# A new order of all pieces, and the last 128 tokens cut at column 352, in a fused attention and SoLU layer

## The chip, the cores and the metric

The kernel runs on one core of one Trainium2 chip. The time is device time in microseconds. Of the kernel before there are three timed runs (178.30, 178.34 and 178.52 us, median 178.34 us) and one profiled execution, from which every view below is taken.

## The reference

Eight batches of eight heads go through a linear attention (no softmax: `k^T v` first, then `q` times that), an RMS norm per head, and then a SoLU layer: a matmul, `h * softmax(h)`, a layer norm, a second matmul.

```python
batch, n_heads, seq, head_dim = (8, 8, 576, 64)     # q, k, v
n_tokens, d_model, d_ff = (4608, 512, 1024)         # w_in, w_out, g_ln

kv = np.einsum('bhsd,bhse->bhde', k, v)
out = np.einsum('bhsd,bhde->bhse', q, kv)
rms = np.sqrt(np.mean(out * out, axis=-1, keepdims=True) + 1e-06)
x = out / rms * g_norm            # then to (batch * seq, heads * head_dim)

h = x @ w_in
e = np.exp(h - np.max(h, axis=-1, keepdims=True))
solu = h * e / (np.sum(e, axis=-1, keepdims=True) + 1e-09)
mu = np.mean(solu, axis=-1, keepdims=True)
var = np.mean((solu - mu) ** 2, axis=-1, keepdims=True)
return ((solu - mu) / np.sqrt(var + 1e-06) * g_ln) @ w_out
```

## The kernel before

The 4608 tokens are nine chunks of 512: chunks 0 to 7 take 512 of the 576 rows of one batch each, and chunk 8 the 64 rows that are left of each batch. A chunk passes through these pieces, whose names are used from here on (the first number is always the chunk or batch):

- `q`, `k`, `v` load a batch (DMAs that POOL issues). `kv_mm.b` is the 72 small matmuls of `k^T v`, and `kv.b.x.part` are the six copies that bring its two banks to SBUF in bf16 (`kv_copy`, recorded at L229; VectorE, or ScalarE where the order says `:act`).
- `qT` turns `q`: for chunks 4 to 8 by a transposing DMA on SyncE's queue, before that by TensorE.
- For each half `hf` of the heads: `o_mm.c.hf` (16 matmuls, 64 for chunk 8; they need `qT` and all copies of `kv`), two squares `sq.c.hf.z` on ScalarE, `oa.c.hf` that adds them (VectorE or POOL, L460), `s_mm.c.hf` (one matmul, the mean over a head, L465), `ln` and `ex` on ScalarE (the inverse root, L472 and L476) and `x.c.hf.z` on VectorE (two instructions each, L489).
- For each of eight blocks `f` of `d_ff`: `h.c.f` (four matmuls of 128x512, L532; in two parts for chunks 0 to 2), `exp.c.f` on ScalarE (L539), `u.c.f` = `h * e` on VectorE (L543), `usq.c.f` = `u * u` (ScalarE or POOL), and for each pair of blocks `es.c.n`, the sum of two `e` (POOL, L551).
- VectorE folds these in halves: `ua.c.0` (2048 columns), `ua.c.1`, `ua.c.2`, the same for `usqa`, and one `esa` (all L575). `sums.c` (16 matmuls, L594) takes the three statistics from them, `turn` and `stats` (VectorE) and `rstd.c` (ScalarE) make the factor of the layer norm.
- `out.c.m` (eight matmuls of 128x512 in two parts, L651) is the second matmul for 128 tokens, `ob.c.m` scales it by `rstd` (`scale`, L239 on ScalarE, L241 on VectorE), `store.c.m` writes it out (two DMAs of 64 rows on SyncE's queue, L679; chunk 8 one DMA, L675). The last 128 tokens, `out.8.3`, are done in two column parts `x` = 0 and 1 with a bank, a scale and a store each (`out_half`, `scale_half`).
- `warm.i` are matmuls on zeros whose result nobody reads; `WARM` gives their numbers.

Nothing is scheduled at run time. The string `ORDER` lists all 919 pieces; `Plan.emit` walks it and calls each piece's function, so it is the program order of every engine at once (`:act`, `:pool` choose an engine where there is a choice). An engine takes its instructions in that order and waits, in place, for what each one needs. `ROOMS` gives a digit for every buffer in the order of first use: which of the 8 PSUM banks, which of the 4 `ob` tiles, and so on. A piece whose room was another's before waits until the last reader of that one is done: a matmul group for the `u`, `ob`, `x` or `ln` that empties its bank, an `ob` for the landing of the store that last read its tile. `Plan.run` adds one more rule: a piece on POOL also waits for the folds and adds of VectorE (`ua`, `usqa`, `esa`, `oa`) that stand ahead of it in `ORDER`.

Of the kernel before, what the change touches and what calls it, by code (L numbers as in the profile page):

```python
# [35 lines left out]
exp.1.6 h.1.7.0 h.1.7.1 kv_mm.2.0 kv.2.0.1:act u.1.2 kv.2.1.1:act sums.0 out.0.2.0 w_center.2 kv.2.1.2:act kv.2.1.0:act
w_center.7 u.1.1 out.0.2.1 out.0.2.2 turn.0 stats.0 u.1.6 kv.2.0.2:act kv.2.0.0:act usq.1.0 o_mm.2.0 exp.1.7 usq.1.4
w_center.6 u.1.7 rstd.0 sq.2.0.1 sq.2.0.0 oa.2.0 o_mm.2.1 sq.2.1.1 out.0.1.0 sq.2.1.0 out.0.1.1 out.0.2.3 out.0.1.2
ua.1.0 ob.0.2:act s_mm.2.0 out.0.1.3 oa.2.1 ln.2.0 ex.2.0 ua.1.1 out.0.0.0 out.0.0.1 out.0.0.2 s_mm.2.1 ln.2.1
out.0.0.3 qT_mm.3.0 es.1.1 usq.1.7:act ob.0.1 ob.0.0:act out.0.3.0 out.0.3.1 x.2.0.1 x.2.0.0 qT.3.0 ex.2.1 kv_mm.3.0  # L40
# [695 lines left out]
```

## Time and profile before

| | us |
|---|---|
| median of three timed runs | 178.34 |
| the profiled execution, device time | 177.03 |
| its span (first to last instruction of the profile) | 175.3 |
| PE busy | 166.1 |
| ScalarE (ACT) busy | 149.4 |
| VectorE (DVE) busy | 147.9 |
| POOL busy | 106.9 |

The profiled execution is 1.31 us shorter than the median of the timed runs, and 1.7 us of it lie around the span. All places below are in microseconds from the span's start. In a row of the timeline the first number is the start, the second the time until the end of the last of the `xN` instructions of the row, and the brackets hold the idle time of that engine just ahead of the row and what ended it. In the window table each engine has its busy time in the stretch. In groups by line, the two numbers behind the first bar are the busy time in all and the mean of one in ns. PEld are the weight loads of TensorE, which run beside its matmuls.

### The profile page before, as it was taken

The numbers are of one execution on the slowest core, as the hardware profiler recorded it, in microseconds if no ns is written. First come the engines' busy times: TensorE is split into PE (matmuls) and PEld (weight loads), VectorE is DVE, ScalarE is ACT, GpSimd is POOL, SyncE is SP. The second block draws the span as 40 slices with busy tenths as digits, with TensorE's granted clock in tenths as the row PEclk, the third lists the DMA queues.
The fourth block names the chain that finished last, engine by engine and source line by source line (L and its number), as shares of the span: only waits on it lengthen the run. The fifth ranks groups of instructions, "written<-read, shape, count | busy, mean of one in ns | idle before, by whom it ended". The sixth has DMA issues, their size and how long they took to land.

```text
span 175.3 us, 4772 instructions
## 1 busy us (share of the span) xinstructions
PE 166.1 (95%) x1866; PEld 80.4 (46%) x1891; DVE 147.9 (84%) x319; ACT 149.4 (85%) x277; POOL 106.9 (61%) x114
## 2 busy tenths in 40 slices
PE   7899998999999998999999999998999999999992
PEld 2454444556464443445435444453454444444451
DVE  2442959999999999899999999999999989988930
ACT  2027699999999998999999999986989999999742
POOL 7943378999390895658656679699085282508000
PEclk9999999999999999999999999999999999999999
DMA  5999999999999697999999657999895513125666
GB/s 154 264 205 212 208 296 350 208 208 208 208 206 197 144 232 193 162 201 200 166 170 215 156 120 98 196 114 129 165 203 124 118 32 85 42 61 120 148 157 238
DMA packets 34623, 30.27 MB, mean 173 GB/s; under 512 B 16288, under 2 KB 28328, under 8 KB 34600
## 3 DMA queue, kind: packets, MB, share of 16 engines
q0 software_dynamic: 17792, 16.71, 56.9%
q1 hardware_dynamic: 16520, 12.86, 31.2%
q10 hardware_dynamic: 288, 0.39, 0.6%
q8 instruction: 15, 0.25, 0.6%
q14 instruction: 8, 0.07, 0.1%
HBM read 32.51 MB, written 9.44 MB: 239 GB/s over the span
## 4 chain that ended last, share of the span: by engine, by line
PE 65%; DVE 15%; ACT 8%; DMA 6%; issue 3%; SPq 1%; POOL 1%; ACTq 0%; POOLq 0%
PE out_ps L651 27%; PE h_ps L532 23%; DVE u_sb L543 5%; DMA k_sb<-in_k_dram 5%; DVE x_sb L489 4%; ACT e_sb L539 3%; PE warm_ps L300 3%; PE o_ps L448 3%; PE sum_ps L594 2%; ACT osq_sb L233 2%; PE s_ps L465 2%; PE kv_ps L375 2%; DVE kvd L229 2%; PE qt_ps L427 2%; DMA out_dram<-ob_sb 1%
## 5 line engine op out<-in xcount | busy, mean ns | idle before, releaser
L532 PE MATMUL h_ps<-x_sb,w_in_sb 128*128 128x512 bf16 x276 | 67.8, 379 | 0.9 <-DVE u_sb L543 0.2
L651 PE MATMUL out_ps<-w_out_sb,u_sb 128*128 128x512 bf16 x270 | 65.8, 379 | 0.6 <-issue 0.2
L551 POOL TENSOR_TENSOR es_sb<-e_sb 128x512 bf16<-128x512 f32 x36 | 45.4, 1279 | 26.0 <-ACT e_sb L539 11.4
L543 DVE TENSOR_TENSOR u_sb<-h_ps,e_sb 128x512 bf16<-128x512 f32 x72 | 46.8, 684 | 3.1 <-ACT e_sb L539 2.8
L539 ACT ACTIVATE e_sb<-h_ps,zero_t 128x512 f32<-128x512 f32 x72 | 46.9, 696 | 1.2 <-PE h_ps L532 0.9
L532 PEld LDWEIGHTS <-w_in_sb 128*128 128x128 bf16 x288 | 26.9, 98 | 33.1 <-issue 2.9
L651 PEld LDWEIGHTS <-u_sb 128*128 128x128 bf16 x280 | 26.3, 98 | 32.3 <-issue 2.2
L489 DVE SCALAR_TENSOR_TENSOR x_sb<-o_ps,g_sb,rst_sb 128x256 bf16<-128x256 f32 x72 | 30.1, 478 | 5.6 <-ACT rst_sb L482 3.5
L235 POOL TENSOR_TENSOR usq_sb<-u_sb 128x512 bf16<-128x512 bf16 x25 | 26.0, 1055 | 13.2 <-DVE usq_sb L575 8.0
L233 ACT ACTIVATE usq_sb<-u_sb,zero_t 128x512 bf16<-128x512 bf16 x47 | 32.2, 717 | 0.0
L233 ACT ACTIVATE osq_sb<-o_ps,zero_t 128x512 bf16<-128x512 f32 x36 | 22.9, 692 | 3.6 <-PE o_ps L448 3.6
L239 ACT ACTIVATE ob_sb<-out_ps,rstd 128x512 f32<-128x512 f32 (+1 forms) x29 | 19.2, 671 | 2.7 <-DMA out_dram<-ob_sb 1.4
L575 DVE TENSOR_TENSOR usq_sb<-usq_sb 128x2048 bf16<-128x2048 bf16 (+2 forms) x24 | 18.7, 778 | 0.7 <-ACT usq_sb L233 0.5
L229 ACT CAST kvd<-kv_ps 64x128 bf16<-64x128 f32 (+3 forms) x36 | 8.2, 241 | 9.8 <-DVE kvd L229 9.4
L300 PE MATMUL warm_ps<-zeros 128*128 128x512 bf16 x42 | 11.9, 427 | 1.3 <-DVE zeros L255 1.2
L476 ACT ACTIVATE rst_sb<-lss_sb,zero_t 128x512 f32<-128x512 f32 x16 | 11.7, 730 | 0.4
L472 ACT ACTIVATE lss_sb<-s_ps,eps_t 128x512 f32<-128x512 f32 x16 | 11.2, 700 | 0.8 <-PE s_ps L465 0.8
L575 DVE TENSOR_TENSOR ua_sb<-u_sb 128x2048 bf16<-128x2048 bf16 x8 | 11.1, 1383 | 0.0
L322 POOL DMA_DIRECT2D q_sb<-in_q_dram x10 | 7.7, 768 | 3.9 <-PE kv_ps L375 2.3
L322 POOL DMA_DIRECT2D k_sb<-in_k_dram x9 | 6.7, 743 | 4.3 <-DVE usq_sb L575 3.5
L375 PEld LDWEIGHTS <-k_sb 64*64 64x64 bf16 x576 | 6.8, 107 | 5.3 <-issue 3.0
L322 POOL DMA_DIRECT2D v_sb<-in_v_dram x9 | 7.1, 791 | 3.4 <-DMA w_in_sb<-in_moe_w_in_dram 1.7
(64 smaller groups left out, 141.1 us busy)
## 6 DMA issues: line engine op xcount, KB each, us to landing
out_dram<-ob_sb SPq DMA_DIRECT2D x65, 128.0 KB, 2.4
k_sb<-in_k_dram POOLq DMA_DIRECT2D x6, 576.0 KB, 13.7
v_sb<-in_v_dram POOLq DMA_DIRECT2D x6, 576.0 KB, 13.5
q_sb<-in_q_dram POOLq DMA_DIRECT2D x6, 512.0 KB, 15.8
u_sb<-in_moe_w_out_dram POOLq DMA_DIRECT2D x2, 1024.0 KB, 15.3
q_sb<-in_q_dram POOLq DMA_DIRECT2D x4, 256.0 KB, 9.9
w_in_sb<-in_moe_w_in_dram POOLq DMA_DIRECT2D x2, 512.0 KB, 12.0
v_sb<-in_v_dram POOLq DMA_DIRECT2D x3, 288.0 KB, 8.3
```

Source lines behind the costliest of these rows:

```text
L233: nc.scalar.activation(out=dst, in_=src, func=AF.Square, bias=zero_t[:, :])
L235: on[engine].tensor_tensor(out=dst, in0=src, in1=src, op=MUL)
L239: nc.scalar.activation(out=dst, in_=src, func=AF.Copy, scale=by)
L300: nc.tensor.matmul(t[:, :], zeros[:, 0:128], zeros[:, :], start=True, stop=True)
L322: nc.gpsimd.dma_start(t.rearrange("p n j d -> p n (j d)")[:, hs.start // 2:hs.stop // 2], rows_of(src, b, hs, js))
L489: nc.vector.scalar_tensor_tensor(out=t[:, 2 * hf + dh, z], in0=T["o", c, hf, z][:, dh], scalar=g_rep[dh], in1=T["rst", c, hf][:, z], op0=M ...
L532: nc.tensor.matmul(bank(("h", c, f), [128, 512])[:, :], w_in_sb[:, dt, f * 128:(f + 1) * 128], T["x", c][:, dt].rearrange("p a b c -> p (a ...
L539: nc.scalar.activation(out=t[:, f % 2, :], in_=T["h", c, f][:, :], func=AF.Exp, bias=zero_t[:, :])
L543: nc.vector.tensor_tensor(out=t[:, f, :], in0=T["h", c, f][:, :], in1=T["e", c, f // 2][:, f % 2, :], op=MUL)
L551: on[engine].tensor_tensor(out=t[:, n, :], in0=e[:, 0, :], in1=e[:, 1, :], op=ADD)
L575: nc.vector.tensor_tensor(out=to[:, 0:n, :], in0=src[:, 0:n, :], in1=src[:, n:2 * n, :], op=ADD)
L651: nc.tensor.matmul(bank(("out", c, m), [128, d_model])[:, :], T["u", c][:, f, m * 128:(m + 1) * 128], w_out_sb[:, f, :], start=(f == 0), s ...
```

## The change

`ORDER` and `ROOMS` are replaced as a whole: the same pieces in another order, with other rooms, and with other engines for some. ScalarE has 40 `kv` copies where it had 36 (VectorE 20 for 24), VectorE makes 13 of the adds `oa` where it made 11 (POOL 3 for 5) and 12 scales `ob` where it made 8 (ScalarE 25 for 29). `WARM` has 43 matmuls where it had 44, in eight groups for seven. The last 128 tokens are cut at column 352 instead of 256, and their first part is scaled by VectorE, the second by ScalarE, where ScalarE scaled both.

```diff
 ORDER = """
...
-ua.8.0 ua.8.1 usqa.8.0 store.6.0 store.6.2 ua.8.2 usqa.8.1 out.8.2.0 esa.8.0 usqa.8.2 ob.7.0:act store.6.1 store.7.0
...
-ob.8.3.0:act ob.8.3.1:act store.8.3.0 store.8.3.1:act
+store.6.2 ua.8.1 ua.8.2 usq.8.0:act usq.8.5:act usq.8.3:act usqa.8.0 usqa.8.1 out.8.2.0 usqa.8.2 out.7.2.1 out.8.2.1
+ob.7.0:act out.7.1.0 out.7.1.1 ob.7.1 ob.7.3:act store.6.1 store.7.0 sums.8 store.7.3 turn.8 ob.7.2:act out.8.0.0
+out.8.1.0 stats.8 rstd.8 out.8.0.1 ob.8.0 ob.8.2:act store.7.2 out.8.1.1 ob.8.1 store.7.1 store.8.2:act store.8.0
+out.8.3.0 store.8.1 ob.8.3.0 store.8.3.0 out.8.3.1 ob.8.3.1:act store.8.3.1:act
 """
...
 WARM = """
-17 6 2 2 9 7 1
+17 8 2 3 5 5 2 1
 """
...
+    ENDS = (slice(0, 352), slice(352, d_model))
+
     def out_half(x):
-        t = bank(("out", LAST, 3, x), [128, d_model // 2])
+        t = bank(("out", LAST, 3, x), [128, ENDS[x].stop - ENDS[x].start])
         for f in range(NF):
             nc.tensor.matmul(
-                t[:, :], T["u", LAST][:, f, 384:512], w_out_sb[:, f, x * d_model // 2:(x + 1) * d_model // 2],
-                start=(f == 0), stop=(f == NF - 1),
+                t[:, :], T["u", LAST][:, f, 384:512], w_out_sb[:, f, ENDS[x]], start=(f == 0), stop=(f == NF - 1),
             )
 
     def scale_half(engine, x):
         t = kept_tile(("ob", LAST, 3), [128, d_model], FP32)
-        times(engine, t[:, x * d_model // 2:(x + 1) * d_model // 2], T["out", LAST, 3, x][:, :], T["rstd", LAST][:, 3:4])
+        times(engine, t[:, ENDS[x]], T["out", LAST, 3, x][:, :], T["rstd", LAST][:, 3:4])
```

What the new order does is seen engine by engine. The number behind a tile tells buffers of the same name apart; a name such as `DMAHW4_49` in brackets is one of the eight semaphores on which the landings of the DMAs that SyncE and ScalarE issue are counted in turn.

**First place: the wait of `ob.1.1` on ScalarE.** SyncE's queue around the stores of chunk 0, before; `ob_sb_1071` is `ob.0.1`, `ob_sb_1035` is `ob.0.2`, and `ob_sb_1468` is `ob.1.3`:

```order
L435 DMA_TRANSPOSE qT_sb_1254<-q_sb_685 128x16x128 [waits DMAHW1_49,DMASW5_49]
L679 DMA out_0_dram<-ob_sb_1071 64x512 [waits DMAHW2_49,DVE_49]
L679 DMA out_0_dram<-ob_sb_1071 64x512 [waits DMAHW3_49]
L679 DMA out_0_dram<-ob_sb_1035 64x512 [waits DMAHW4_49]
L679 DMA out_0_dram<-ob_sb_1035 64x512 [waits DMAHW5_49]
L679 DMA out_0_dram<-ob_sb_1468 64x512 [waits DMAHW6_49,Activation_49]
```

The queue has the same sequence in the change. What differs is on ScalarE, before; `ob_sb_1525` is `ob.1.1`, the squares into `osq_sb_1494` are `sq.4.0`, those into `osq_sb_1527` are `sq.4.1`:

```order
L239 ACTIVATE ob_sb_1468<-out_ps_1448,rstd_1350 128x512 [waits DMAHW5_49,DMAHW4_49,PE_49]
L233 ACTIVATE osq_sb_1494<-o_ps_1478,zero_t_81 128x2x256 [waits PE_49,Pool_49]
L233 ACTIVATE osq_sb_1494<-o_ps_1476,zero_t_81 128x2x256
L233 ACTIVATE usq_sb_1252<-u_sb_1233,zero_t_81 128x512 [waits DVE_49]
L239 ACTIVATE ob_sb_1525<-out_ps_1470,rstd_1350 128x512 [waits DMAHW5_49,DMAHW4_49,PE_49]
L233 ACTIVATE osq_sb_1527<-o_ps_1500,zero_t_81 128x2x256
L539 ACTIVATE e_sb_1540<-h_ps_1535,zero_t_81 128x512 [waits PE_49]
L472 ACTIVATE lss_sb_1551<-s_ps_1549,eps_t_79 128x512 [waits PE_49]
```

And ScalarE at the same place with the change, where `ob_sb_1529` is `ob.1.1`:

```order
L239 ACTIVATE ob_sb_1469<-out_ps_1440,rstd_1449 128x512 [waits DMAHW5_49,DMAHW4_49,PE_49]
L233 ACTIVATE osq_sb_1498<-o_ps_1480,zero_t_81 128x2x256 [waits PE_49,Pool_49]
L233 ACTIVATE osq_sb_1498<-o_ps_1478,zero_t_81 128x2x256
L233 ACTIVATE osq_sb_1521<-o_ps_1505,zero_t_81 128x2x256 [waits PE_49]
L233 ACTIVATE usq_sb_1259<-u_sb_1251,zero_t_81 128x512 [waits DVE_49]
L239 ACTIVATE ob_sb_1529<-out_ps_1471,rstd_1449 128x512 [waits DMAHW3_49,DMAHW2_49,PE_49]
L539 ACTIVATE e_sb_1553<-h_ps_1548,zero_t_81 128x512 [waits PE_49,Pool_49]
L472 ACTIVATE lss_sb_1561<-s_ps_1559,eps_t_79 128x512 [waits PE_49]
```

`ob.1.1` takes the tile of `ob.0.1` instead of that of `ob.0.2`: it waits for the store that SyncE issues one pair earlier (the pair on DMAHW2 and DMAHW3), and it stands behind one more square. The bank that `s_mm.4.0` writes was that of `out.1.1`, emptied by `ob.1.1`; with the change it is that of `out.1.3`, emptied by `ob.1.3`.

**Second place: the copies of `kv.7`.** VectorE from `kv.7.0.1` to `kv.7.0.0`, before; the tiles `u_sb_2301` are `u.6`, `ua_sb_2458` is `ua.5.0`:

```order
L229 CAST kvd_7_0_1_152<-kv_ps_2333 64x128 [waits PE_49]
L543 TENSOR_TENSOR u_sb_2301<-h_ps_2318,e_sb_2316 128x512 [waits Activation_49]
L601 STREAM_TRANSPOSE sum_ps_2410<-sum_ps_2410 128x128 [waits PE_49]
L229 CAST kvd_7_0_2_153<-kv_ps_2333 64x128
L606 TENSOR_TENSOR w_2447<-sum_ps_2410,factors_94 128x4x2 [waits DVE_49]
L607 MEMSET w_2447 128x4
L609 TENSOR_TENSOR terms_2450<-sum_ps_2410,w_2447 128x12 [waits DVE_49]
L611 TENSOR_REDUCE vare_2452<-terms_2450 128x4 [waits DVE_49]
L575 TENSOR_TENSOR ua_sb_2458<-u_sb_2048 128x2048
L543 TENSOR_TENSOR u_sb_2301<-h_ps_2427,e_sb_2434 128x512 [waits Activation_49]
L543 TENSOR_TENSOR u_sb_2301<-h_ps_2442,e_sb_2329 128x512 [waits Activation_49]
L229 CAST kvd_7_0_0_151<-kv_ps_2333 128x128
```

ScalarE with the change, where all six copies of `kv.7` stand:

```order
L539 ACTIVATE e_sb_2317<-h_ps_2320,zero_t_81 128x512 [waits PE_49]
L229 CAST kvd_7_1_2_156<-kv_ps_2330 64x128 [waits PE_49]
L229 CAST kvd_7_0_0_151<-kv_ps_2327 128x128
L229 CAST kvd_7_1_1_155<-kv_ps_2330 64x128
L229 CAST kvd_7_1_0_154<-kv_ps_2330 128x128
L539 ACTIVATE e_sb_2433<-h_ps_2428,zero_t_81 128x512 [waits PE_49,Pool_49]
L229 CAST kvd_7_0_1_152<-kv_ps_2327 64x128
L239 ACTIVATE ob_sb_2439<-out_ps_2147,rstd_2231 128x512 [waits DMAHW6_49,DMAHW1_49,DMAHW7_49,DMAHW0_49,DVE_49]
L539 ACTIVATE e_sb_2307<-h_ps_2449,zero_t_81 128x512 [waits PE_49]
L539 ACTIVATE e_sb_2433<-h_ps_2460,zero_t_81 128x512 [waits PE_49]
L229 CAST kvd_7_0_2_153<-kv_ps_2327 64x128
```

Three copies leave VectorE, the last of them from behind `ua.5.0` and two `u.6`; on ScalarE the last of the six stands behind `exp.6.3`, `ob.3.2`, `exp.6.6` and `exp.6.2`. `o_mm.7.1` follows `out.4.1` on TensorE in both.

**Third place: `esa.4.0` on VectorE.** Before, with `usqa.3.1` first, then `oa.6.0` (`osq_sb_2107`), `esa.3.0`, `ua.3.2`, and `esa.4.0` (`es_sb_1876`):

```order
L543 TENSOR_TENSOR u_sb_2048<-h_ps_2062,e_sb_2067 128x512 [waits Activation_49]
L575 TENSOR_TENSOR usq_sb_1596<-usq_sb_1596 128x1024 [waits DVE_49]
L460 TENSOR_TENSOR osq_sb_2107<-osq_sb_2107 128x512 [waits Activation_49]
L575 TENSOR_TENSOR es_sb_1650<-es_sb_1650 128x1024
L575 TENSOR_TENSOR ua_sb_1838<-ua_sb_1838 128x512
L575 TENSOR_TENSOR es_sb_1876<-es_sb_1876 128x1024 [waits Pool_49]
```

With the change, where `es_sb_1911` is `esa.4.0` and `osq_sb_2085` is `oa.6.0`:

```order
L543 TENSOR_TENSOR u_sb_2105<-h_ps_2047,e_sb_2065 128x512 [waits Activation_49]
L575 TENSOR_TENSOR es_sb_1911<-es_sb_1911 128x1024 [waits Pool_49]
L460 TENSOR_TENSOR osq_sb_2085<-osq_sb_2085 128x512 [waits DVE_49,Activation_49]
L575 TENSOR_TENSOR ua_sb_1857<-ua_sb_1857 128x512 [waits DVE_49]
L575 TENSOR_TENSOR usq_sb_1590<-usq_sb_1590 128x1024 [waits DVE_49]
L575 TENSOR_TENSOR usq_sb_1590<-usq_sb_1590 128x512 [waits DVE_49]
```

`esa.4.0`, which waits for the last `es.4` of POOL, has moved ahead of `oa.6.0`, for which `s_mm.6.0` waits. On POOL the pieces ahead of it are `es.4.1`, `es.4.0`, `usq.4.1` before, and `es.4.1`, `usq.4.1`, `es.4.0` with the change.

More of the change, by code (lines that the diff above doesn't have):

```diff
@@ L36 @@
[L36 to L40, printed above, removed]
```

137 lines of the change are left out of this document (70 added, 67 removed).

## The prediction

> **What bounds the kernel now.** I read the busy shares first, then the table of windows, then the chain that ended last, to see which stretch has time to give.
>
> ```profile
> PE 166.1 (95%) x1866; PEld 80.4 (46%) x1891; DVE 147.9 (84%) x319; ACT 149.4 (85%) x277; POOL 106.9 (61%) x114
> 60.00:65.00 5.00, 4.95 (x93) 2.38 (x92) 4.86 (x12) 4.92 (x11) 5.00 (x5) 1.00 1.12 231
> 65.00:70.00 5.00, 4.24 (x48) 1.83 (x48) 4.70 (x10) 4.13 (x8) 3.20 (x4) 1.00 0.96 171
> 120.00:125.00 5.00, 4.40 (x50) 1.98 (x50) 5.00 (x9) 3.60 (x9) 2.63 (x3) 1.00 0.91 181
> 150.00:155.00 5.00, 5.00 (x25) 2.29 (x24) 4.45 (x11) 4.75 (x10) 2.27 (x2) 1.00 0.01 3
> 145.61 3.45 PE h_ps L532 x16
> ```
>
> In a window row come the length and then the busy time of PE, PEld, DVE, ACT and POOL; the 1.00 behind them is the granted clock, which is full throughout. The last row, from the chain, is sixteen matmuls in 3.45 us, 0.216 us each. PE is busy in nearly every stretch, and from about 25 us DVE and ACT are too (4.86 and 4.92 of 5 at 60 to 65). So no reordering shortens the work itself: it can give back waits. PE has few of them: two stretches stand out, 65 to 70 (4.24) and 120 to 125 (4.40). The beginning and the last 3 us are the other places.
>
> The Trainium skill's page "Perfetto Trace Analysis", section "Identifying the Most-Contended Engine", says that matmul busy time is a bad measure and that the busy share of the weight loads tells TensorE's headroom. That share is 46% here, so by the page ACT (85%) and DVE (84%) would be the contended engines. The trace agrees only in part: at 0.216 us a matmul without a gap, PE has nothing to give in 150 to 155, while DVE is full where PE is not, in 120 to 125. What the sum would be by the page's rule stands with the third rival.
>
> **The change part by part.** The sum is made against the profiled execution, 177.03 us with a span of 175.3.
>
> *First place, `ob.1.1`.*
>
> ```profile
> 67.52 0.72 ACT L233 ACTIVATE usq_sb<-u_sb,zero_t 128x512 bf16<-128x512 bf16 x1
> 69.08 0.69 ACT L239 ACTIVATE ob_sb<-out_ps,rstd 128x512 f32<-128x512 f32 x1 [0.83 <-DMA out_dram<-ob_sb]
> 69.82 0.38 PE L465 MATMUL s_ps<-osq_sb,head_mean 128*128 128x512 bf16 x1 [0.71 <-ACT ob_sb L239]
> 72.28 1.66 DVE L489 SCALAR_TENSOR_TENSOR x_sb<-o_ps,g_sb,rst_sb 128x256 bf16<-128x256 f32 x4 [0.64 <-ACT rst_sb L476]
> 64.81 1.10 SPq L679
> 66.60 2.37 DMA out_dram<-ob_sb
> ```
>
> ACT stood 0.83 us before `ob.1.1` until the second half of `store.0.2`, issued at 66.60, had landed 2.37 us later; PE lost 0.71 behind it, DVE 0.64. With the change `ob.1.1` waits for `store.0.1`, whose second half is the issue at 64.81: with the same 2.37 us it lands between 67.2 (from the start of that issue) and 68.3 (from its end). ACT reaches `ob.1.1` after `usq.2.0` (end 68.24) and one square more; if that takes as long as `usq.2.0`, at about 68.9. The wait is covered. `s_mm.4.0` no longer depends on it. All three engines are full around this place, so they gain together what the least of them lost: 0.64 us; bounds 0 (another wait comes instead) and 0.83. I take **-0.65**. Next late there is `h.3.6`, whose bank `ob.1.1` now empties: PE does `out.1.1.1`, `out.1.2`, `h.3.2`, `s_mm.4.0` first, more than 3 us of matmuls behind `o_mm.4`, and `ob.1.1` ends in less.
>
> *Second place, `kv.7`.*
>
> ```profile
> 117.58 0.32 DVE L601 STREAM_TRANSPOSE sum_ps<-sum_ps 128x128 f32<-128x128 f32 x1
> 118.65 0.17 DVE L611 TENSOR_REDUCE vare<-terms 128x4 f32<-128x12 f32 x1
> 117.43 0.69 ACT L539 ACTIVATE e_sb<-h_ps,zero_t 128x512 f32<-128x512 f32 x1 [0.55 <-PE h_ps L532]
> 118.73 2.01 DVE L575 TENSOR_TENSOR ua_sb<-u_sb 128x2048 bf16<-128x2048 bf16 x1
> 121.86 0.27 DVE L229 CAST kvd<-kv_ps 128x128 bf16<-128x128 f32 x1
> 122.19 0.65 PE L448 MATMUL o_ps<-qT_sb,kvd 64*32 64x256 bf16 x32 [0.55 <-DVE kvd L229]
> 122.70 1.84 ACT L233 ACTIVATE osq_sb<-o_ps,zero_t 128x512 bf16<-128x512 f32 x3 [1.34 <-PE o_ps L448]
> L229 DVE CAST kvd<-kv_ps 64x128 bf16<-64x128 f32 x9 | 2.6, 287 | 0.2
> L229 ACT CAST kvd<-kv_ps 64x128 bf16<-64x128 f32 x15 | 3.7, 260 | 0.2
> 95.93 3.10 DVE L543 TENSOR_TENSOR u_sb<-h_ps,e_sb 128x512 bf16<-128x512 f32 x5
> 94.17 1.23 DVE L575 TENSOR_TENSOR usq_sb<-usq_sb 128x2048 bf16<-128x2048 bf16 x1
> ```
>
> The first two rows are the beginning of `turn.4` and the end of `stats.4`, with one copy between: 1.24 us, 0.96 without it. `o_mm.7.1` waited 0.55 us for the last copy, which stood on a full DVE behind a fold of 2.01 us and two `u`. The change takes three copies, 3 x 0.28 = 0.84 us, off DVE and adds about as much to ACT, which idled 0.55 and 1.34 there. On ACT six copies of 0.26 us and four `exp` or `ob` of 0.69 are 4.3 us from `kv_mm.7.0` to the last copy, whereas PE has four `h` and `out.4.1` to do, 24 matmuls or 5.2 us. The copies are then in time; the next late thing is the bank of `o_mm.7.0`, emptied by `u.6.1`, and that of `o_mm.7.1`, by `u.6.6`: DVE does `u.6.4`, the fold, `turn.4`, `stats.4` and three `u` first, at 0.62 us a `u` (five in 3.10) 0.6 + 2.0 + 1.0 + 1.9 = 5.5 us. If `exp.6.4` lets it begin 0.5 us after `kv_mm.7.0`, it is done at 6.0, against PE's 5.2 + 0.3 for `sums.4`. That leaves 0.5 us of the wait if the fold is as slow again, and none if it takes 1.23 like the other fold above. Bounds -0.55 and 0; I take **-0.4**.
>
> *A smaller wait of the same kind.*
>
> ```profile
> 88.27 1.89 PE L532 MATMUL h_ps<-x_sb,w_in_sb 128*128 128x512 bf16 x8 [0.19 <-DVE u_sb L543]
> ```
>
> `h.4.1` waited for `u.4.5`. In the new order five matmul groups of chunk 4 and `h.4.0` lie between, and ACT's copies of `kv.5` come earlier. Most of it should go: **-0.15**, bounds -0.19 and 0.
>
> *The beginning.*
>
> ```profile
> 13.85 2.12 PE L300 MATMUL warm_ps<-zeros 128*128 128x512 bf16 x9
> 16.30 0.60 PE L465 MATMUL s_ps<-osq_sb,head_mean 128*128 128x512 bf16 x2
> 19.37 0.59 PE L532 MATMUL h_ps<-x_sb,w_in_sb 128*128 128x512 bf16 x2
> 20.53 1.02 PE L532 MATMUL h_ps<-x_sb,w_in_sb 128*128 128x512 bf16 x4
> 21.48 0.43 PE L448 MATMUL o_ps<-qT_sb,kvd 64*32 64x256 bf16 x16
> 24.62 0.38 PE L465 MATMUL s_ps<-osq_sb,head_mean 128*128 128x512 bf16 x1 [0.23 <-POOL osq_sb L460]
> L460 DVE TENSOR_TENSOR osq_sb<-osq_sb 128x512 bf16<-128x512 bf16 x11 | 4.6, 420 | 0.2
> ```
>
> POOL issues the loads in the same order, only `ident` behind one more of them, so the data come as before. `s_mm.0.0` moves ahead of the matmuls of `kv.1` and has five warm matmuls ahead of it, not nine; but `s_mm.0.1` comes later, since ACT has two copies of `kv.1` ahead of its square, and the first `h` follows it: I get the first `h` at the same 19 us. By `o_mm.1.0` (21.48) PE then has four half `h` done, not three (6 matmuls above): -0.43. The 0.23 us at `s_mm.1.0` goes, because `oa.1.0` is made by DVE (0.42 us there) and not by POOL. Against that, three warm matmuls stand behind the first `h` where one stood, and the one before is in the time above already: +3 x 0.216 = 0.65. Together **0**, bounds -0.6 and +0.6.
>
> *The end.*
>
> ```profile
> 171.50 1.00 ACT L239 ACTIVATE ob_sb<-out_ps,rstd 128x256 f32<-128x256 f32 x2 [0.53 <-DMA out_dram<-ob_sb]
> 172.03 0.47 ACT ob_sb L239
> L239 ACT ACTIVATE ob_sb<-out_ps,rstd 128x512 f32<-128x512 f32 x27 | 18.2, 686 | 2.1 <-PE out_ps L651 1.1 <-DMA out_dram<-ob_sb 0.8
> L241 DVE TENSOR_SCALAR ob_sb<-out_ps,rstd 128x512 f32<-128x512 f32 x8 | 5.9, 745 | 0.9 <-PE out_ps L651 0.9
> 170.25 1.76 PE out_ps L659 x16
> 166.35 0.34 PE sum_ps L594 x16
> ```
>
> The last matmul ends at 172.0, ACT scales 256 columns in 0.47 us, the store and the close take the rest. Between 512 columns (0.686) and 256 (0.47) a column costs 0.83 ns: 160 columns 0.39, **-0.1**. The eight pairs of matmuls keep 512 columns a pair (1.76 us); if the weight loads bounded the eight narrow ones at a full 128 rows' 0.1 us, +0.25. DVE has the first 352 columns, at most the 0.745 us of a whole scale there, about 0.55 us before the last matmul: hidden.
>
> *What else moves* lies beside other work: four copies more on ACT, four scales more on DVE behind 140 us (4.45 of 5 at 150), two adds more.
>
> *New waits.* Some 900 pieces stand in a new sequence. Followed through the places above and the rival below, two have less than 0.3 us of cover. In the execution before, the waits of PE quoted above for 30 to 170 us are 0.71 + 0.55 + 0.19 = 1.45 us; a new order may have none or as many. I take **+0.5**, bounds 0 and +1.5.
>
> Sum: -0.65 - 0.4 - 0.15 + 0 - 0.1 + 0.5 = **-0.8 us**, 176.2 in a profiled execution. The timed runs lie 1.31 us above it, a distance I keep: 178.34 - 0.8 = **177.5 us**.
>
> **The rivals.**
>
> *Slower: `esa.4.0` holds up DVE.*
>
> ```profile
> 95.54 2.50 POOL L551 TENSOR_TENSOR es_sb<-e_sb 128x512 bf16<-128x512 f32 x2 [1.71 <-ACT usq_sb L233]
> 97.99 1.05 POOL L235 TENSOR_TENSOR usq_sb<-u_sb 128x512 bf16<-128x512 bf16 x1
> 100.82 0.69 DVE L575 TENSOR_TENSOR es_sb<-es_sb 128x1024 bf16<-128x1024 bf16 x1
> ```
>
> Before, `es.4.0` was done at 98.04 and `esa.4.0` came at 100.82: 2.8 us of cover. Now `usq.4.1` stands ahead of `es.4.0`, and POOL needs 2.50 + 1.05 = 3.55 us behind `usqa.3.0`, while DVE has five `u` and two copies, 5 x 0.62 + 2 x 0.28 = 3.66 us. The cover is 0.1. From there each microsecond that POOL is late stops DVE, then `oa.6.0`, then `s_mm.6.0`. The lateness can be up to the two POOL pieces behind which `es.4.1` might wait, 2.1 us. It decides from 1.2 us on: there the forecast's gain is gone and the loss can be measured. Halfway from 1.2 to 2.1 the time is 177.5 + 1.6 = **179.1**.
>
> *No change: the waits only move.* PE, ACT and DVE are full on both sides of each place, so PE's saving may meet the next load or turned `q`: `o_mm.6` waits for a transposing DMA that stands in SyncE's queue behind `store.2.3`, which did not move. Then only the end is kept: **178.2**.
>
> *A larger gain, by DVE's account.* If DVE sets the pace from 25 to 125 us, the three copies count in full, and with no new waits: -0.64 - 0.84 - 0.1 = -1.6, **176.8**. DVE's 5.00 at 120 to 125 speaks for it; PE's gapless pace while DVE has 4.45, later, speaks against it. The Trainium skill's rule on the contended engine, above, leads here as well.
>
> **How the numbers follow.** Forecast 0.42 (its own range 177.0 to 178.0), larger gain 0.18, no change 0.18, slower 0.22. The range 176.4 to 179.0 leaves out the ends of the larger gain and the upper part of the slower case, together about 0.2. A measurement can tell about 0.2%, 0.36 us, from no change: faster 0.60, same 0.18, slower 0.22.
>
> **What would show it.** In the profile of the changed kernel: no wait of ACT on a store at `ob.1.1`, and none of PE at `s_mm.4.0`; at most 0.3 us ahead of `o_mm.7.1`; the first `h` at 19 us; a last scale of 0.39 us. I am wrong if PE shows a new wait of a microsecond, first of all at `s_mm.6.0`, or if `o_mm.1.0` stands later than 21.5 with fewer than four half `h` done.

## The result, and the profile after

| | before | with the change |
|---|---|---|
| median of the timed runs, us | 178.42 (4 runs, 178.30 to 178.52) | 176.06 (4 runs, 175.46 to 176.76) |
| profiled execution, device time, us | 177.03 | 176.05 |
| its span, us | 175.3 | 174.2 |

The ratio of the comparison is 0.9896, with a 95% interval of 0.9858 to 0.9934: faster by about 1.0%. On another chip (the run `after_again` below) it was 0.9907 (0.9872 to 0.9941). The forecast was -0.84 us, a ratio of 0.9953. In one of the runs below, `turn_first_before`, two of the twelve executions showed a lower granted clock (0.987 and 0.989) and took 180.12 and 180.53 us; its median leaves them out.

The busy shares and the windows of the changed kernel:

```profile
PE 167.6 (96%) x1890; PEld 80.3 (46%) x1890; DVE 149.2 (86%) x321; ACT 148.5 (85%) x277; POOL 104.8 (60%) x112
65.00:70.00 5.00, 5.00 (x54) 2.24 (x53) 4.68 (x8) 4.97 (x9) 3.31 (x4) 1.00 0.66 146
80.00:85.00 5.00, 4.83 (x53) 2.15 (x52) 4.69 (x14) 4.42 (x10) 4.57 (x4) 1.00 1.15 199
85.00:90.00 5.00, 4.53 (x22) 2.00 (x21) 4.24 (x7) 4.97 (x10) 1.31 (x2) 1.00 0.93 157
95.00:100.00 5.00, 4.97 (x53) 2.31 (x52) 4.89 (x11) 4.95 (x10) 3.50 (x3) 1.00 0.84 194
120.00:125.00 5.00, 4.92 (x53) 2.09 (x51) 4.15 (x7) 4.94 (x11) 1.64 (x2) 1.00 1.11 187
```

65 to 70 has gone from 4.24 to 5.00 of TensorE, and 120 to 125 from 4.40 to 4.92. But 80 to 90 now has two waits. The busy sums of the two profiles can't be subtracted to find the gain: the profile of before lacks some 25 matmul records (1866 of PE beside 1891 weight loads), that of after none.

So I compared the two by TensorE's lag: the start of a weight load, minus the usual length of all the pieces ahead of it in TensorE's order (one value for each kind of piece, 0.216 us for a matmul of 512 columns, the same for both kernels). Where the lag grows, TensorE lost time. The lag of after minus that of before:

| at, us | 55 | 70 | 76 | 90 | 120 | 125 | 135 | 165 |
|---|---|---|---|---|---|---|---|---|
| difference, us | -0.01 | -0.94 | -0.75 | -0.30 | -0.31 | -0.64 | -0.80 | -0.81 |

One warm matmul fewer adds -0.22, which makes the -1.02 by which `sums.8` comes earlier (166.28 before, 165.26 after), and the last scale adds -0.08: the -1.1 of the span. In this pair of executions the first place gave 0.93, a wait of `h.3.1` at 71 us took back 0.19, two waits between 80 and 90 another 0.45, the second place gave 0.33, and a stretch behind it 0.16. The rows of the places, in the changed kernel:

```profile
67.86 0.73 ACT L233 ACTIVATE usq_sb<-u_sb,zero_t 128x512 bf16<-128x512 bf16 x1
68.48 0.70 ACT L239 ACTIVATE ob_sb<-out_ps,rstd 128x512 f32<-128x512 f32 x1
68.66 0.38 PE L465 MATMUL s_ps<-osq_sb,head_mean 128*128 128x512 bf16 x1
...
70.06 0.68 DVE L543 TENSOR_TENSOR u_sb<-h_ps,e_sb 128x512 bf16<-128x512 f32 x1
70.80 0.53 PEld L532 LDWEIGHTS <-w_in_sb 128*128 128x128 bf16 x3 [0.31 <-issue]
...
83.33 0.28 DVE L229 CAST kvd<-kv_ps 128x128 bf16<-128x128 f32 x1
83.71 0.65 PE L448 MATMUL o_ps<-qT_sb,kvd 64*32 64x256 bf16 x32 [0.17 <-ACT rstd L617]
84.55 0.69 ACT L239 ACTIVATE ob_sb<-out_ps,rstd 128x512 f32<-128x512 f32 x1 [0.50 <-DMA out_dram<-ob_sb]
86.28 1.27 ACT L539 ACTIVATE e_sb<-h_ps,zero_t 128x512 f32<-128x512 f32 x2
87.01 1.29 DVE L543 TENSOR_TENSOR u_sb<-h_ps,e_sb 128x512 bf16<-128x512 f32 x2 [0.15 <-ACT e_sb L539]
87.75 1.89 PE L532 MATMUL h_ps<-x_sb,w_in_sb 128*128 128x512 bf16 x8 [0.47 <-DVE u_sb L543]
...
116.61 1.22 DVE L575 TENSOR_TENSOR ua_sb<-u_sb 128x2048 bf16<-128x2048 bf16 x1
120.09 0.69 ACT L539 ACTIVATE e_sb<-h_ps,zero_t 128x512 f32<-128x512 f32 x1
120.81 1.29 DVE L543 TENSOR_TENSOR u_sb<-h_ps,e_sb 128x512 bf16<-128x512 f32 x2 [0.87 <-ACT e_sb L539]
121.05 0.93 PE L448 MATMUL o_ps<-qT_sb,kvd 64*32 64x256 bf16 x32
...
171.01 0.39 ACT L239 ACTIVATE ob_sb<-out_ps,rstd 128x160 f32<-128x160 f32 x1 [2.65 <-PE out_ps L661]
```

The first three rows are the first place: `ob.1.1` starts the moment ScalarE is free, and `s_mm.4.0` follows without a gap. The next two are the small wait at 71 us: `h.3.1` takes the bank that `u.3.2` empties, and `u.3.2` ends at 70.74. The six rows from 83.33 to 87.75 hold two waits. `o_mm.5` stood 0.17 us; its row names `rstd`, but the last copy of `kv.5` (the first of the six) ends at 83.61, later than `rstd` at 83.48, and the matmuls need it. And `ob.2.2` stood 0.50 us for the landing of `store.1.2`, whose tile it takes (`ob.2.2` took that of `ob.0.1` before); behind it `exp.4.5` came late, then `u.4.5`, which empties the bank of `h.4.3`, and TensorE idled 0.47 us at `h.4.3`. The four behind them are the second place: the fold `ua.5.0` takes 1.22 us where it took 2.01, but DVE now waits 0.87 us for `exp.6.1`, whose `u.6.1` empties the bank of `o_mm.7.0`; those 32 matmuls take 0.93 us where they took 0.65.

### The profile page after: what moved, and what is told of

The parts are those of the page before. It is cut to its first block, busy times and chain, and to the rows that moved or that the text cites. A ratio compares the mean times of both kernels' runs of the same rounds, so it can differ in the third digit from the quotient of the medians.

```text
span 174.2 us, 4804 instructions
## 1 busy us (share of the span) xinstructions
PE 167.6 (96%) x1890; PEld 80.3 (46%) x1890; DVE 149.2 (86%) x321; ACT 148.5 (85%) x277; POOL 104.8 (60%) x112
## 4 chain that ended last, share of the span: by engine, by line
PE 72%; DMA 10%; ACT 9%; POOL 3%; issue 2%; DVE 1%; SPq 0%; ACTq 0%; POOLq 0%
PE out_ps L651 32%; PE h_ps L532 27%; DMA q_sb<-in_q_dram 7%; ACT e_sb L539 4%; DMA out_dram<-ob_sb 4%; PE o_ps L448 3%; PE kv_ps L375 2%; PE sum_ps L594 2%; PE s_ps L465 2%; PE qt_ps L427 2%; ACT ob_sb L239 1%; ACT usq_sb L233 1%; PE mean_ps L632 1%; PE out_ps L661 1%; POOL q_sb L322 1%
## 5 line engine op out<-in xcount | busy, mean ns | idle before, releaser
L532 PE MATMUL h_ps<-x_sb,w_in_sb 128*128 128x512 bf16 x288 | 68.6, 379 | 0.6 <-DVE u_sb L543 0.5
L651 PE MATMUL out_ps<-w_out_sb,u_sb 128*128 128x512 bf16 x280 | 66.8, 379 | 0.0
L239 ACT ACTIVATE ob_sb<-out_ps,rstd 128x512 f32<-128x512 f32 (+1 forms) x25 | 16.7, 678 | 3.3 <-PE out_ps L661 2.7
L229 ACT CAST kvd<-kv_ps 64x128 bf16<-64x128 f32 (+3 forms) x40 | 9.7, 242 | 10.2 <-PE kv_ps L375 6.3
L300 PE MATMUL warm_ps<-zeros 128*128 128x512 bf16 x43 | 12.5, 432 | 1.2 <-DVE zeros L255 1.2
L241 DVE TENSOR_SCALAR ob_sb<-out_ps,rstd 128x512 f32<-128x512 f32 (+1 forms) x12 | 8.7, 731 | 2.4 <-PE out_ps L651 1.9
L575 DVE TENSOR_TENSOR ua_sb<-u_sb 128x2048 bf16<-128x2048 bf16 x8 | 9.7, 1216 | 0.0
```

The source lines that it names most:

```text
L239: nc.scalar.activation(out=dst, in_=src, func=AF.Copy, scale=by)
L300: nc.tensor.matmul(t[:, :], zeros[:, 0:128], zeros[:, :], start=True, stop=True)
L532: nc.tensor.matmul(bank(("h", c, f), [128, 512])[:, :], w_in_sb[:, dt, f * 128:(f + 1) * 128], T["x", c][:, dt].rearrange("p a b c -> p (a ...
L575: nc.vector.tensor_tensor(out=to[:, 0:n, :], in0=src[:, 0:n, :], in1=src[:, n:2 * n, :], op=ADD)
L651: nc.tensor.matmul(bank(("out", c, m), [128, d_model])[:, :], T["u", c][:, f, m * 128:(m + 1) * 128], w_out_sb[:, f, :], start=(f == 0), s ...
```

## The experiments

All times are medians in us; a ratio is to the kernel before on the same chip, with its 95% interval.

| run | of kernel | time (runs) | ratio | profiled span |
|---|---|---|---|---|
| first_alone | before | 176.59 (9) | 0.9938 (0.9912 to 0.9963) | 174.2 |
| second_alone | before | 177.28 (12) | 0.9987 (0.9960 to 1.0015) | 176.4 |
| three_parts | before | 176.08 (12) | 0.9929 (0.9900 to 0.9957) | 174.6 |
| turn_first_before | before | 176.90 (10) | 0.9996 (0.9959 to 1.0033) | 175.0 |
| after_again | after | 175.65 (6) | 0.9907 (0.9872 to 0.9941) | 173.4 |
| first_undone | after | 175.96 (6) | 0.9912 (0.9877 to 0.9947) | 174.0 |
| ob22_tile | after | 175.65 (6) | 0.9887 (0.9856 to 0.9919) | 174.3 |
| turn_first | after | 175.83 (9) | 0.9921 (0.9892 to 0.9951) | 173.2 |
| both_moves | after | 175.43 (8) | 0.9907 (0.9873 to 0.9941) | 173.5 |
| no_late_warm | after | 175.75 (12) | 0.9919 (0.9887 to 0.9951) | 174.5 |
| tail_256 | after | 175.98 (1) | | 174.2 |
| two_fixes | after | 175.23 (6) | 0.9878 (0.9846 to 0.9910) | 173.4 |

The kernel before had medians of 177.52, 177.17, 177.33 and 177.81 on the four chips of these runs (76 runs, 176.35 to 178.51). Nearly all intervals here are some 0.6% wide; what is smaller is read from the profiles.

### The first place alone

```diff
-qT.4 h.2.4.0 usq.2.5 qT.5 store.0.1 store.0.2 h.2.4.1 exp.2.4
+qT.4 h.2.4.0 usq.2.5 qT.5 store.0.2 store.0.1 h.2.4.1 exp.2.4
```

> The kernel before with one edit: store.0.2 and store.0.1 change places in ORDER, so that ob.1.1 waits for the earlier of the two pairs of stores. If the stall at ob.1.1 is worth what the first term says, ScalarE no longer idles at about 69 us, the 0.71 us of TensorE ahead of s_mm.4.0 are gone, and the span falls from 175.3 by 0.65 to 0.9, to 174.4 to 174.7 (ratio 0.995 to 0.996). If waits only move, the idle time of TensorE turns up again at the next piece that waits, before 90 us, and the span stays within 0.2 of 175.3. If VectorE sets the pace, the gain is what VectorE lost there, 0.64.

The kernel before with two stores exchanged, in its profile:

```profile
67.89 0.68 ACT L239 ACTIVATE ob_sb<-out_ps,rstd 128x512 f32<-128x512 f32 x1
68.70 0.38 PE L465 MATMUL s_ps<-osq_sb,head_mean 128*128 128x512 bf16 x1
```

The 0.83 of ScalarE and the 0.71 of TensorE are gone. The lag falls by 0.87 from 55 to 70 us against before, and it stays away to the end; the median falls by 0.93. That is the upper end of the 0.65 to 0.9 expected, a little over the bound of 0.83 in the forecast, and over the 0.64 of VectorE's account. The waits did not move: this one exchange is more than half of what the whole change brings.

### The second place alone

```diff
-kv_mm.7.0 kv.7.1.0:act kv.7.1.1:act kv.7.0.1 sums.4
+kv_mm.7.0 kv.7.1.0:act kv.7.0.0:act kv.7.1.1:act kv.7.0.1:act sums.4
...
-kv.7.0.2 h.6.6.0 stats.4
+kv.7.0.2:act h.6.6.0 stats.4
...
-u.6.6 kv.7.0.0 rstd.4
+u.6.6 rstd.4
```

> The kernel before with one edit: the three copies of kv.7 that VectorE made are made by ScalarE, the big one right behind kv.7.1.0. If the forecast's second term is right, the wait of 0.55 us ahead of o_mm.7.1 shrinks to between 0 and 0.25 and the span falls by 0.3 to 0.55 (ratio 0.997 to 0.998). By VectorE's account the three copies count in full: -0.84 us. If ScalarE's queue makes the last copy late instead, o_mm.7.1 waits as long as before and nothing is gained.

The place in this run's profile:

```profile
118.96 1.05 POOL L235 TENSOR_TENSOR usq_sb<-u_sb 128x512 bf16<-128x512 bf16 x1
119.20 2.76 DVE L575 TENSOR_TENSOR ua_sb<-u_sb 128x2048 bf16<-128x2048 bf16 x1
121.50 2.36 POOL L235 TENSOR_TENSOR usq_sb<-u_sb 128x512 bf16<-128x512 bf16 x2
121.88 2.47 DVE L543 TENSOR_TENSOR u_sb<-h_ps,e_sb 128x512 bf16<-128x512 f32 x4
122.79 1.07 PE L448 MATMUL o_ps<-qT_sb,kvd 64*32 64x256 bf16 x32
```

`o_mm.7.1` no longer waits for a copy, but VectorE gained nothing: with two copies fewer ahead of it the fold begins earlier, beside more of POOL's `usq`, and takes 2.76 us. The `u` behind it are late, the matmuls of `o_mm.7` wait for their banks instead, and the lag grows by 0.79 from 120 to 125 us where it grew by 0.98 before: -0.2. The median's -0.24 can't be told from no change. This run does not decide the account by which every microsecond off VectorE counts (-0.84): the longer fold put 0.75 us back on VectorE. The changed kernel speaks against it. There the three copies are gone and the fold takes 0.79 us less, some 1.6 us off VectorE, and TensorE gained 0.33. The profile of this run is 1.1 us longer than that of before for reasons further ahead: from start to start TensorE lost 0.87 us at `o_mm.4` and 1.43 at `s_mm.4.0`. So the first place has no fixed price: in the profiles that still have it TensorE lost 0.87 us (before), 1.43 (here) and 0.46 (`turn_first_before`).

### The first place undone in the changed kernel

```diff
-h.2.7.0 qT.4 qT.5 store.0.1 usqa.1.1
+h.2.7.0 qT.4 qT.5 store.0.2 store.0.1 usqa.1.1
...
-ob.1.1:act store.0.2 store.1.3
+ob.1.1:act store.1.3
```

> The changed kernel with one edit: store.0.2 stands right ahead of store.0.1, so that ob.1.1 waits for the later of the two pairs again. The second pair landed at 69.14 in the changed kernel and ob.1.1 began at 68.48, so ScalarE should stand about 0.66 us. If a stall of a full ScalarE goes through to the end whatever else is in order, the span rises from 174.2 by 0.5 to 0.7. If the loss of before came through the bank of s_mm.4.0, which ob.1.1 emptied then and does not now, TensorE has 3 us of matmuls behind it and the span rises by less than 0.2.

```profile
67.57 0.74 ACT L233 ACTIVATE usq_sb<-u_sb,zero_t 128x512 bf16<-128x512 bf16 x1
68.57 0.69 ACT L239 ACTIVATE ob_sb<-out_ps,rstd 128x512 f32<-128x512 f32 x1 [0.27 <-PE h_ps L532]
```

This tells little. I had misread the landings: 69.14 was that of `store.1.3`, and the second pair of chunk 0 lands at about 67.8 in the changed kernel. So ScalarE stood only 0.27 us (until 68.57; the row names a matmul, but the second half of `store.0.1`, here the later pair, landed at 68.47), TensorE had lost about 0.1 more than in the profile of after by the end, and the time did not change. That the bank of `s_mm.4.0` matters by itself is left open; the first experiment carries the first place.

### The new wait of the change taken away

`ORDER` stays, and the digits of the ob tiles 1 and 3 are exchanged in `ROOMS` from `ob.2.2` on; written with the pieces that they belong to:

```diff
-ob.2.2 3, ob.2.3 1, ob.2.1 0, ob.2.0 1, ob.3.3 0
+ob.2.2 1, ob.2.3 3, ob.2.1 0, ob.2.0 3, ob.3.3 0
...
```

> The changed kernel with the ob tiles 1 and 3 exchanged from ob.2.2 on, so that ob.2.2 waits for the store of ob.0.2, long done, and not for that of ob.1.2, which landed at 84.45 and stopped ScalarE for 0.50 us at 84.05. If that stop, through exp.4.5 and u.4.5, is what makes h.4.3 late at 86.9 us (TensorE idle 0.47 in the groups, 0.63 from start to start), the wait ahead of h.4.3 falls to 0.1 to 0.2 and the span falls from 174.2 by 0.4 to 0.6. If VectorE is the cause (ua.3.0 and oa.5.1 ahead of u.4.5), the wait stays and the gain is under 0.15.

```profile
66.09 0.65 PE L448 MATMUL o_ps<-qT_sb,kvd 64*32 64x256 bf16 x32 [0.62 <-DMA qT_sb<-q_sb]
...
84.50 0.68 ACT L239 ACTIVATE ob_sb<-out_ps,rstd 128x512 f32<-128x512 f32 x1
86.94 1.29 DVE L543 TENSOR_TENSOR u_sb<-h_ps,e_sb 128x512 bf16<-128x512 f32 x2
87.69 1.02 PE L532 MATMUL h_ps<-x_sb,w_in_sb 128*128 128x512 bf16 x4
```

`ob.2.2` begins without a wait, and so does `h.4.3`: the chain from the store over `exp.4.5` and `u.4.5` was the cause, not VectorE. The span is nevertheless that of the change, since this execution had another wait, of 0.62 us, which the profile of after did not have: `o_mm.4` stood for the transposing DMA of `q.4`.

### Is the transposing DMA what makes executions differ?

Three runs ask this: the changed kernel unaltered, and one edit in both kernels, here in the changed one:

```diff
-ob.0.3:act h.2.4.0 h.2.4.1 store.0.3 store.0.0 h.2.7.0 qT.4 qT.5 store.0.1
+ob.0.3:act h.2.4.0 h.2.4.1 qT.4 store.0.3 store.0.0 h.2.7.0 qT.5 store.0.1
```

> The changed kernel unaltered, to see how far its executions scatter. In the traces so far the transposing DMA of q.4 was issued at 59.45 to 60.57 us (one of the four store issues ahead of it takes 0.9 to 2.0 us instead of 0.6) and landed at 63.5 to 64.0 where it was issued before 60.0 and at 66.1 to 66.3 where it was issued later; then o_mm.4 waited 0.8 us. If that is what makes executions differ, a profile shows one case or the other, and times lie in two groups about 0.7 us apart, 175.4 to 176.8. If the change is worth what the forecast said on top of a fixed distance, the ratio is 0.995; by the traces it is 0.989 to 0.991.

> The changed kernel with one edit: qT.4 stands ahead of store.0.3 and store.0.0 in ORDER, so that the transposing DMA is issued at 56 to 57 us, not behind four store issues of which one is slow. If its late landing is what makes some executions longer, o_mm.4 waits in none, the spread falls under 0.8 us, and the median falls by 0.2 to 0.6 against the unaltered kernel of the same chip. If the stores, now 1.9 us later, hold up ob.1.0 or ob.1.3 instead (they wait for the landings of store.0.0 and store.0.3), VectorE or ScalarE idles at 64 to 66 us and nothing is gained.

> The kernel before with the same edit (qT.4 ahead of store.0.3). In its late case o_mm.4 waits 0.9 us, and the stores of SyncE's queue come 0.6 us later, so that ob.1.1 waits 1.4 us more of which TensorE lost 1.43: about 1.3 us more than in the profiled execution of 177.03, which is the distance of 1.31 us that the forecast kept. If the distance is this, the median falls to 177.0 +- 0.3, or by 0.5 to 1.3 against the kernel before. If the distance is something that every execution has outside the profile, the median stays within 0.3.

The executions of the changed kernel scatter over 175.18 to 176.22, those of `turn_first` over 174.96 to 176.67 although `o_mm.4` waits for nothing in its profile, and neither median falls clear of the scatter (175.83 against 175.65, and 176.90 against 177.17). In the old order the edit also makes waits of its own: in its profile `ob.1.0` stood 0.27 us for a store that now comes later, and then `o_mm.4` 0.34 for copies of VectorE. So the late transposing DMA is at most one source of scatter among others, and as the reason for the distance of 1.31 us it falls. There is no fixed distance: the runs of the kernel before on the other chips lie at 176.35 to 178.51, with the profiled 177.03 among them; the 178.30 to 178.52 of the first chip were the upper end.

What scatters in the profiles are three places where a DMA comes just in time. From the starts of successive matmuls, in nine profiles of the changed order, TensorE lost 0 to 0.78 us at `qT_mm.1.0` (for `q.1.0`), 0.09 or, in one, 0.79 at `o_mm.4`, and 0.16 to 0.63 at `h.4.3` in the six in which `ob.2.2` keeps its tile.

### Both of these edits

> The changed kernel with qT.4 ahead of store.0.3 and with the exchange of ob tiles 1 and 3 from ob.2.2 on. If the two gains are independent (0.2 to 0.6 from the transposing DMA, 0.4 to 0.5 from h.4.3), the median is 0.6 to 1.0 below the unaltered changed kernel, at a ratio of 0.983 to 0.987. If ScalarE and VectorE are the bound between 65 and 90 us, the second gain is lost to other waits and the ratio is that of the first edit alone.

175.43 against 175.65 on the same chip: less than was expected, and within the scatter. Its profile shows neither wait.

### The late warm matmuls

```diff
-17 8 2 3 5 5 2 1
+17 8 2 3 5 5 0 0
```

> The changed kernel without the last two groups of warm matmuls (warm.6 and warm.7, three matmuls of 0.216 us on zeros, result unread). The forecast put three late warm matmuls at +0.65 us on the path. If TensorE's order is what counts there, the span falls by 0.6. If the loads set the pace of the beginning (k.1.1 landed at 26.17 us, kv_mm.1.1 began at 26.47, behind warm.6), the matmuls only fill a wait: the lag of TensorE at 30 us stays within 0.2 and so does the time. If the clock needs them, the granted clock falls below 1.0 or matmuls take longer than 0.216 us, and the time rises.

```profile
26.14 0.76 PE L375 MATMUL kv_ps<-v_sb,k_sb 64*64 64x64 bf16 x36
27.89 0.43 PE L448 MATMUL o_ps<-qT_sb,kvd 64*32 64x256 bf16 x16 [0.34 <-ACT kvd L229]
```

Where the warm matmuls stood, `o_mm.1.1` waits for copies of `kv.1.1`, whose matmuls begin at 26.14, with the last of its loads. The time is that of the change (175.75). From the start of `qT_mm.1.1` to that of `h.0.5.1` TensorE took 4.15 us, and 4.42 or 4.43 in the eight other profiles of the changed order: 0.28 of their 0.65 us is saved, and more than half of it filled a wait. Counting all of it on the path was too much; the granted clock of the profiled execution is 0.997.

### The cut at column 352

```diff
-    ENDS = (slice(0, 352), slice(352, d_model))
+    ENDS = (slice(0, 256), slice(256, d_model))
```

> The changed kernel with the last 128 tokens cut at column 256 again, both engines as in the change (VectorE the first part, ScalarE the second). By the forecast's fifth term the last scale takes 0.47 us where it took 0.39 and the end comes 0.08 to 0.1 us later behind the last matmul; the sixteen matmuls take the same 1.9 us. If the narrow matmuls of the changed kernel are bounded by weight loads, the sixteen take up to 0.25 us less here.

```profile
169.02 1.91 PE L661 MATMUL out_ps<-w_out_sb,u_sb 128*128 128x256 bf16 x16
170.97 0.47 ACT L239 ACTIVATE ob_sb<-out_ps,rstd 128x256 f32<-128x256 f32 x1 [2.65 <-PE out_ps L661]
```

0.47 us for 256 columns, 0.39 for 160, and 1.91 us for the sixteen matmuls with either cut: the term of 0.08 to 0.1 us holds.

### Three local edits in the old order

The kernel before with the diffs of `first_alone` and `second_alone`, and

```diff
-ob.8.3.0:act ob.8.3.1:act store.8.3.0 store.8.3.1:act
+ob.8.3.0 ob.8.3.1:act store.8.3.0 store.8.3.1:act
...
-        t = bank(("out", LAST, 3, x), [128, d_model // 2])
+        t = bank(("out", LAST, 3, x), [128, (352, 160)[x]])
```

with the columns of the last matmuls, scales and stores to match.

> The kernel before with its old order and three local edits: store.0.2 ahead of store.0.1 (worth 1.1 us alone, ratio 0.9938), the six copies of kv.7 on ScalarE (0.2 us alone), and the last 128 tokens cut at column 352 with the first scale on VectorE (0.08 us). If these three are the change's gain and the rest of the new order gives as much as it takes, the sum is 1.3 to 1.4 us and the ratio 0.992 to 0.9925, within 0.2% of the changed kernel's 0.9907. If the new order's beginning or its other places carry a gain of their own, the changed kernel stays 0.3 us or more below this one (ratio 0.9935 or more here). If the parts cover one another, the ratio is that of the first edit alone, 0.994.

0.9929, between the two readings: above the 0.992 to 0.9925 of the first and below the 0.9935 of the second. Exchanging two stores, moving three copies and cutting at 352 brings the old order to within 0.22% of the changed one, and the two intervals overlap. In its profile the fold `ua.5.0` took 2.73 us, much as in `second_alone`. Whether the rest of the new order is worth something of its own can't be told from these runs.

### Both waits of the changed kernel mended

`ob22_tile`'s edit again, and the second place: banks 4 and 6 are exchanged in `ROOMS` from `o_mm.7.0` on (so that it follows `h.6.2` and not `h.6.1`), and in `ORDER`:

```diff
-exp.6.1 u.6.1 usq.5.4:act o_mm.7.1 o_mm.7.0 store.3.2 u.6.2 usqa.5.0
+exp.6.1 u.6.2 usq.5.4:act o_mm.7.1 o_mm.7.0 store.3.2 u.6.1 usqa.5.0
```

> The changed kernel with two edits: the ob tiles 1 and 3 exchanged from ob.2.2 on (as in ob22_tile), and for the second place the banks 4 and 6 exchanged from o_mm.7.0 on, with u.6.2 ahead of u.6.1 on VectorE. In the changed kernel o_mm.7.0 took the bank that u.6.1 empties, and u.6.1 waited 0.87 us for exp.6.1; TensorE lost 0.35 between o_mm.7.1 and o_mm.7.0. With the edit it takes the bank that u.6.2 empties, whose exp.6.2 ends 1 us earlier. If ScalarE's exp.6.1 is the next late thing, the 0.35 at 121 us is gone and so are the 0.16 to 0.63 at 86.5; the median falls by 0.4 to 0.7 against the unaltered changed kernel, to a ratio of 0.986 to 0.988. If PE's saving only meets the next load, turned q or bank, the waits appear behind 122 us and the ratio stays at 0.990.

```profile
85.43 1.28 ACT L539 ACTIVATE e_sb<-h_ps,zero_t 128x512 f32<-128x512 f32 x2
86.91 0.81 PE L532 MATMUL h_ps<-x_sb,w_in_sb 128*128 128x512 bf16 x3
...
120.27 0.64 PE L448 MATMUL o_ps<-qT_sb,kvd 64*32 64x256 bf16 x32
120.85 1.90 PE L651 MATMUL out_ps<-w_out_sb,u_sb 128*128 128x512 bf16 x8
```

Both waits are gone and no other came behind 122 us: `o_mm.7` takes 0.64 us again where it took 0.93. So `exp.6.1` was what stood next behind the copies. The median is 175.23 at a ratio of 0.9878, 0.42 us under the 175.65 of the unaltered changed kernel on another chip. It is the lowest of all these runs and well under the kernel before; that it beats the changed kernel is likely from the two waits, but the intervals of the ratios overlap.

## Why the prediction was right, and which sizes were off

The direction and the mechanism were right: the change gives back waits at the places named, and shortens no work. The gain was undershot: -0.84 us foretold, -1.65 to -1.86 us by the ratios of 0.9907 (of 177.17) and 0.9896 (of 178.42), -0.98 by the profiled executions. The median of the first four timed runs, 176.06, lies 0.34 us under the low end of the range. The waits read below account for the gain between the two profiles; where the other 0.7 us of the timed gain lies is not shown. Part of it can be the first place, whose price differs between executions.

- **First place, -0.65.** Right in mechanism, with no wait left and `s_mm.4.0` on time; too small. It measured -0.93 between the two profiles and by the medians of `first_alone`. The step that was off is "they gain together what the least of them lost: 0.64". TensorE is the engine that is full to the end, and what it lost counts: 0.71 idle, 0.87 from start to start. VectorE's smaller loss was no bound.
- **Second place, -0.4.** -0.33 measured. The fold took 1.22 us, for which I had put the rest of the wait at zero; about a third of a microsecond stayed all the same, because `exp.6.1` stood behind the copies on ScalarE. I had asked what is late next on VectorE only. The bank was named rightly: that of `o_mm.7.0`, emptied by `u.6.1`.
- **The smaller wait, -0.15.** Wrong at this place: it grew. `u.4.5` still empties a bank that TensorE needs soon (now that of `h.4.3`), and 0.19 became 0.47. I followed the bank and not ScalarE, where `ob.2.2` had got a tile whose store was issued 6 us before and took 6.4 us to land.
- **New waits, +0.5.** A fair size: the waits at 71 us and between 80 and 90 took 0.65, the smaller one's growth included. The largest of them, at `ob.2.2`, is the change's own mistake, of the same kind as the one that it mends at the first place.
- **The beginning, 0.** The lag is the same at 55 us, and one warm matmul fewer is the 0.22. The first `h` came earlier than the 19 us foretold, and `o_mm.1.0` had four halves of `h` ahead of it, as foretold:

```profile
18.36 0.59 PE L532 MATMUL h_ps<-x_sb,w_in_sb 128*128 128x512 bf16 x2
19.46 0.62 PE L427 MATMUL qt_ps<-ident,q_sb 128*128 128x128 bf16 x8 [0.50 <-DMA q_sb<-in_q_dram]
19.91 1.46 PE L532 MATMUL h_ps<-x_sb,w_in_sb 128*128 128x512 bf16 x6
21.30 0.43 PE L448 MATMUL o_ps<-qT_sb,kvd 64*32 64x256 bf16 x16
```

   But the 0.6 us were lost to the load of `q.1.0`, and the terms of -0.43 and +0.65 that I added up to nothing were not what happened: the loads set this stretch.
- **The end, -0.1.** -0.08, as the last scale of 0.39 us shows.
- **The distance of 1.31 us.** The step "a distance I keep" failed. Executions of the kernel before differ by up to 2.2 us, so one profiled execution and three timed runs say little about a distance. That is why 177.5 was too high while the sum of the terms, 176.2, is near the 176.05 of the profile after. That nearness is in part luck. The first place gave 0.28 us more than its term, and the warm matmul (0.22) and the stretch behind the second place (0.16) had none; the smaller wait and the new ones took 0.3 more than forecast.

The slower rival did not come, though its cover was even thinner than the 0.1 us that I gave it. The last `es.4` of POOL and the `u` of VectorE ahead of `esa.4.0`, in the changed kernel:

```profile
96.61 1.89 DVE L543 TENSOR_TENSOR u_sb<-h_ps,e_sb 128x512 bf16<-128x512 f32 x3
97.25 1.27 POOL L551 TENSOR_TENSOR es_sb<-e_sb 128x512 bf16<-128x512 f32 x1
98.56 0.69 DVE L575 TENSOR_TENSOR es_sb<-es_sb 128x1024 bf16<-128x1024 bf16 x1
```

VectorE is done at 98.50, POOL at 98.52, and `esa.4.0` begins at 98.56. The third rival's size (-1.6) came nearest to the timed gain, but not its reason: at the second place some 1.6 us came off VectorE, which then stood 0.87 us for `exp.6.1`, and TensorE gained 0.33. The rule of the Trainium skill that led there ("Perfetto Trace Analysis", "Identifying the Most-Contended Engine"), read by the weight-load share of 46% alone, did not hold at these places: what counted was TensorE's own loss. The section names MFU, the share of the peak arithmetic rate, beside that share; the forecast left it out.

## What to carry to other kernels

A tile taken again too soon after its store was issued stops an engine that has nothing to do with the store; look for such pairs first, since exchanging two of them, or two buffers, costs nothing and was worth more here than moving work between engines. Where a wait goes, ask what is late next on every engine that the waiting piece needs, not on the one that was late before. And where runs scatter by 2 us, sum a forecast against the profiled execution, and take many runs of both kernels for the distance.
